# Seven-product layers on one core: more of the sums formed in PSUM, and a new order of the products

## The chip, the cores and the metric

The kernel runs on one core of one Trainium2 chip. The metric is the device time of one execution in microseconds (us). Everything is fp32. The engines are TensorE (PE, with its weight loads as PEld), VectorE (DVE), ScalarE (ACT), GpSimd (POOL) and SyncE (SP), whose queue issues nearly all DMAs.

## The reference

The computation is attention with a threshold, then a Fourier mix with a two-layer channel block on its output (batch 8, 8 heads, 576 rows, 64 columns per head, so 512 columns in all and 2048 hidden ones):

```
scores = q @ k^T / 8; keep those >= max - tau; attn = softmax; x = attn @ v
u  = x + real(fft(fft(x, axis=seq), axis=dim))
un = (u - mean(u)) / sqrt(var(u) + 1e-6)
out = u + relu(un @ w_ch1) @ w_ch2
```

## The kernel before

The attention is worked in 160 steps of 128 query rows for two heads (`scores`, `softmax_first/second/third`, `weights_in_parts`, `values_in_parts`). In each step PE forms scores into a pair of two-bank PSUM tiles (tag `sc`), DVE takes the row maximum (L506), ACT the exponential (L512), DVE the threshold and the sum (L527), ACT the scaling (L540). PE then transposes the weights: one transpose into a tile `pe`, and four into each of two tiles `pw` (L578, L596), which ACT copies out (L584, L598).

The channel block takes 512 rows at a time, in nine groups. Group 0 is multiplied in the ordinary way (`channels`), and in its second half the weights are combined into the left sides of seven-product (Strassen-Winograd) multiplication and stored to device memory in blocks (`w1_forms`, tensor `f1`, 28 blocks; `w2_forms`, tensor `f2`, 49 blocks). Groups 1 to 8 run in `two_level`, called g below. Its first layer has four *parts* of 512 columns; a part has seven *products* of two 256-row halves, 28 in all. Each is a generator step that ends in a `yield`, and is one matmul group of 1.73 us on PE; I call its place in the order a *slot*, 0 to 27. The right sides `t1`, `t2`, `minus_t4`, `t3` are differences of the tokens (`u_form`, L1087). Per part, with P1 to P7 the products, what the layer needs is

```
h00 = relu(P1 + P2)        h01 = relu(P1 + P6 + P5 + P3)
h10 = relu(P1 + P6 + P7 + P4)   h11 = relu(P1 + P6 + P7 + P5)
```

Before the change the order in a part is 1, 2, 5, 6, 4, 7, 3. Products 6 and 7 accumulate on the bank of product 1 (`sum_`); all others take a bank of their own. ACT copies P1, P5, P4 out (L1172, L1174, L1182). DVE adds P2 to `h00`, the bank to `h11` giving `h01`, the bank to both halves `h10, h11` in one 1024-column instruction (`both`, `twice`), and P3 to `h01`: four additions that read PSUM, all on L1100. Three `relu` instructions on ACT follow (L1105). `s1_part` (POOL, L1109) then adds `h01` and `h11`. In the second layer the products have seven inner products each (`L1`, `J`), in two banks per outer product (L1306). Product 1 is copied out by ACT (L1321) and product 2 added to it by DVE (L1323).

All engines run in the order in which the program was written out by hand: `fill` advances the channel block by as many slots as a running budget allows, three times in each attention step, so that about one slot lies between the pieces of the attention. The budget counts what a `yield` reports, 4096 for every slot. Groups 7 and 8 have little or no attention left beside them. All single-bank PSUM tiles, of the attention and of the channel block alike, share the tag `mm` with four buffers. A new tile gets, of the buffers whose last reader was already written out in the program, the one whose last reader came first: in the compiled program 947 of 963 such tiles follow this rule exactly. If that reader has not finished when PE gets there, PE waits.

Of the kernel before, what the change touches and what calls it, by code (L numbers as in the profile page):

```python
# [47 lines left out]
def kernel(  # L48
# [12 lines left out]
    nc = tc.nc  # L61
# [856 lines left out]

    ORDER = (1, 2, 5, 6, 4, 7, 3)
    L1 = (1, 2, 5, 4, 6, 7, 3)
    J = (1, 2, 5, 4, 6, 7, 3)
    HH = HID // 2
# [3 lines left out]
    def w1_forms():  # L928

        quarters = {  # L930
            (i, k): [w1[2 * k + c][:, HH * i : HH * (i + 1)] for c in range(2)]
            for i in range(2) for k in range(2)
        }

        def keep(m, at):
            to = f1[:, :, :].rearrange("p (part m) (c n) -> p m c part n", m=7, c=2)
            for c in range(2):
                nc.sync.dma_start(
                    out=to[:, ORDER.index(m), c],
                    in_=quarters[at][c].rearrange("p (part n) -> p part n", n=256),  # L940
                )

        def form(out_, in0, in1, op=ALU.subtract):
            for c in range(2):
                nc.vector.tensor_tensor(
                    out=quarters[out_][c], in0=quarters[in0][c], in1=quarters[in1][c], op=op
                )
                yield

        keep(1, (0, 0))  # L950
        keep(4, (1, 1))
        yield
        keep(2, (0, 1))
        yield
        yield from form((1, 1), (1, 1), (1, 0), ALU.add)
        keep(5, (1, 1))
        yield from form((1, 0), (0, 0), (1, 0))
        keep(7, (1, 0))
        yield from form((0, 0), (1, 1), (0, 0))
        keep(6, (0, 0))  # L960
        yield from form((0, 1), (0, 1), (0, 0))
        keep(3, (0, 1))
        for _ in range(4):
            yield
        ensure(0)
# [96 lines left out]
    def two_level(g, rows):  # L1062
# [21 lines left out]

        def u_form(out_, in0, in1):
            for c in range(2):
                (nc.vector if g >= NG - 2 else nc.gpsimd).tensor_tensor(  # L1087
                    out=out_[:, c], in0=in0[:, c], in1=in1[:, c], op=ALU.subtract
                )

# [54 lines left out]
                yield  # L1145

        own = l2_forms(1)
        for part in range(4):
            cols = slice(512 * part, 512 * part + 512)
            h00, h01, h10, h11 = (quadrant(k, i)[:, cols] for k in range(2) for i in range(2))  # L1150
            both = hs[:, 4096:8192].rearrange("p (i n) -> p i n", i=2)[:, :, cols]
            sum_ = None
            for at, m in enumerate(ORDER):
                left = block(g, False, 7 * part + at)
                if m in (6, 7):
                    bank = sum_
                else:
                    bank = ps.tile([128, 512], FP32, tag="mm", bufs=4, name="ph")
                if m == 1:
                    sum_ = bank  # L1160
                for q in range(2):
                    for c in range(2):
                        nc.tensor.matmul(  # L1163
                            bank[:, 256 * q : 256 * q + 256].rearrange(
                                "p (two n) -> p two n", two=2
                            ),
                            left[:, 256 * c + 128 * q : 256 * c + 128 * q + 128], right[m][:, c],
                            start=q == 0 and c == 0 and m not in (6, 7), stop=c == 1,
                            skip_group_check=True,
                        )  # L1170
                if m == 1:
                    nc.scalar.copy(h00, bank[:, :])  # L1172
                elif m == 5:
                    nc.scalar.copy(h11, bank[:, :])  # L1174
                elif m == 2:
                    add(h00, bank[:, :])
                    relu(h00)
                    background()
                elif m == 6:
                    add(h01, bank[:, :], h11)  # L1180
                elif m == 4:
                    nc.scalar.copy(h10, bank[:, :])  # L1182
                    background()
                elif m == 7:
                    twice = bass.AP(
                        tensor=bank.tensor, offset=bank.offset,
                        ap=[list(bank.ap[0]), [0, 2], [1, 512]],
                    )
                    add(both, twice)
                    relu(both)  # L1190
                else:
                    add(h01, bank[:, :])
                    relu(h01)
                next(forms, None)
                tick()
                if part == 3 and g > 1 and at in (2, 3, 5):
                    next(own)
                yield 4096
            if g > 1:
                s1_part(part)  # L1200
        for _ in forms:
            pass
        while pending or held:
# [72 lines left out]
        if g < NG - 1:  # L1276
            at_slots(6, (0, 1), [plus(P, v_22, v_u), plus(P, v_21, v_u)])
        else:
            at_slots(6, (0, 0), [plus(V, v_22, v_u), plus(P, v_21, v_u)])
            at_slots(6, (1, 1, 1, 1, 1), gather(V, v_22))  # L1280
            at_slots(6, (2, 2), finish(1, 1, v_22))
            at_slots(6, (2, 2, 3, 3, 3), gather(V, v_21))
            at_slots(6, (4, 4), finish(1, 0, v_21))
            at_slots(6, (4,), [stores(2, 3)])
            w = v_12.rearrange("p (j n) -> p j n", n=128)
            at_slots(6, (4,) * 4, [
                plus(V, w[:, 1:5:3], twice(w[:, 0])), plus(V, w[:, 6], w[:, 2]),
                plus(V, w[:, 6], w[:, 4]), lambda: rows.add(0, slice(256, 384), w[:, 1]),
            ])
            second = bass.AP(  # L1290
                tensor=w.tensor, offset=w[:, 3].offset, ap=[list(w.ap[0]), [-128, 2], [1, 128]]
            )
            at_slots(6, (5,) * 4, [
                plus(V, w[:, 5], w[:, 4]), plus(V, w[:, 2:4], twice(w[:, 5])),
                lambda: rows.add(1, slice(256, 512), second), stores(1),
            ])
        for at, m in enumerate(L1):
            for jn, j in enumerate(J):
                cut = g == NG - 1 and m == 3
                if jn in (0, 4) or cut and jn > 4:  # L1300
                    bank = ps.tile([128, 512], FP32, tag="mm", bufs=4, name="po")
                c0 = 0 if cut and jn > 4 else 128 * (jn % 4)
                to = bank[:, c0 : c0 + 128]
                right_ = block(g, True, 7 * at + jn)
                for s in range(4):
                    nc.tensor.matmul(  # L1306
                        to, lefts[m][j][:, s], right_[:, 128 * s : 128 * (s + 1)],
                        start=(jn in (0, 4) or cut and jn > 4) and s == 0, stop=s == 3,
                        skip_group_check=True,
                    )  # L1310
                if jn in (3, 6) or cut and jn > 3:
                    first, end = (0, 512) if jn == 3 else (512, NV)
                    if cut and jn > 3:
                        first, end = 128 * jn, 128 * jn + 128
                    src = bank[:, 0 : end - first]

                    def here(v):
                        return v[:, first:end]

                    if m in (1, 5, 4):  # L1320
                        nc.scalar.copy(here({1: v_u, 5: v_22, 4: v_21}[m]), src)  # L1321
                    elif m == 2:
                        V.tensor_tensor(out=here(v_11), in0=here(v_u), in1=src, op=ALU.add)  # L1323
                    else:
                        to = here(v_12 if m == 3 else v_u)
                        V.tensor_tensor(out=to, in0=to, in1=src, op=ALU.add)  # L1326
                while held:
                    held.pop(0)()
                held.extend(side.get((at, jn), ()))
                while held and not holding:  # L1330
                    held.pop(0)()
                if jn == 3 and at < 4:
                    rows.load((2, 3, 0, 1)[at])
                    if at == 3:
                        wanted.append(rows)
                    yield ND * 128
                if jn < 6:
                    yield 2048
            background()
            if m != 3:  # L1340
                yield 2048
# [37 lines left out]
    def background():  # L1379

        if late:
            fold_more()
# [361 lines left out]
```

## Time and profile before

| what | value |
|---|---|
| median of 3 runs | 1605.03 us (1603.99 to 1605.74) |
| profiled execution, its time | 1605.7 us |
| span of its instructions | 1603.8 us |
| PE, DVE, ACT, POOL busy | 1537.4, 1105.6, 908.4, 811.7 us |
| first layers of groups 1 to 8 begin at | 386.8, 551.7, 726.9, 900.3, 1074.0, 1247.6, 1400.5, 1498.7 us |
| first layers end at | 460.4, 630.8, 806.8, 979.5, 1153.1, 1326.7, 1452.8, 1547.3 us |

The profile is of one execution; 1.9 us of its time lie outside the span. A line of a group of instructions reads: source line, engine, operation, tile written <- tiles read, shape, count | busy us in total, mean ns of one | idle time of the engine just before them, and what ended most of it. PE's matmuls are pipelined, and the end of a record is modelled: a product of 1.73 us is eight records that overlap. Records carry the tile's name in the program, so `w_all` also stands for rooms that are cut out of the second weight buffer.

### The profile page before, as it was taken

What the parts mean: (1) busy time and instruction counts of PE and PEld (TensorE: products, weight loads), DVE (VectorE), ACT (ScalarE), POOL (GpSimd) and SP (SyncE); (2) the same over time, 40 slices, a digit from 0 to 9 for tenths busy, and PEclk for the clock granted to TensorE, in tenths of its full rate; (3) what the DMA queues carried; (4) which work ended last, traced back from release to release, by engine and by line L of the source; (5) the groups of instructions that cost most, each with busy time, mean ns of one, the idle gap of its engine ahead of it and who ended that gap; (6) DMA issues with size and microseconds to landing.
All of it is one profiled execution on the core that took longest, in us unless ns stands there. A gap on an engine that the chain in (4) does not pass through costs nothing.

```text
span 1603.8 us, 27061 instructions
## 1 busy us (share of the span) xinstructions
PE 1537.4 (96%) x9770; PEld 1189.2 (74%) x9770; DVE 1105.6 (69%) x2165; ACT 908.4 (57%) x1873; POOL 811.7 (51%) x1014
## 2 busy tenths in 40 slices
PE   8999979999999999999999999999999999999997
PEld 4555445555787778877787878787887778879997
DVE  7997886845869566766577566856676656746547
ACT  5774665554655666656666666656665665223121
POOL 6784664034455552536254724455263625537646
PEclk9999999999999999999999999999999999999998
DMA  6423221555956264634564355626463534546655
GB/s 158 131 57 115 75 76 36 175 158 164 291 159 203 72 182 125 182 104 141 141 175 140 113 159 145 191 69 180 123 185 108 154 113 158 191 157 237 235 193 190
DMA packets 245499, 239.05 MB, mean 149 GB/s; under 512 B 196947, under 2 KB 214869, under 8 KB 225014
## 3 DMA queue, kind: packets, MB, share of 16 engines
q1 hardware_dynamic: 242854, 237.02, 49.1%
q8 instruction: 78, 1.28, 0.3%
q10 hardware_dynamic: 2512, 0.30, 0.2%
q14 instruction: 55, 0.45, 0.1%
HBM read 207.50 MB, written 29.62 MB: 148 GB/s over the span
## 4 chain that ended last, share of the span: by engine, by line
PE 76%; DVE 14%; ACT 4%; issue 2%; POOL 2%; DMA 1%; SPq 0%; DVEq 0%; ACTq 0%; POOLq 0%
PE ph L1163 24%; PE po L1306 17%; PE pv L627 8%; PE sc L427 7%; PE pw L596 6%; PE po L901 4%; PE ph L877 2%; PE py L750 2%; DVE e L467 2%; PE sc L433 1%; PE pa L767 1%; PE pe L578 1%; PE pa L771 1%; DVE neg L451 1%; ACT e L512 1%
## 5 line engine op out<-in xcount | busy, mean ns | idle before, releaser
L512 ACT ACTIVATE e<-sc,neg 128x576 f32<-128x576 f32 x216 | 158.6, 734 | 139.8 <-DVE neg L506 139.4
L506 DVE TENSOR_REDUCE neg<-sc 128x1 f32<-128x576 f32 x216 | 154.0, 749 | 112.0 <-PE sc L427 104.1
L1306 PE MATMUL po<-w,w_all 128*128 128x128 f32 x1792 | 229.1, 278 | 0.7 <-ACT ends L584 0.7
L1306 PEld LDWEIGHTS po<-w,w_all 128*128 128x128 f32 x1792 | 214.7, 193 | 10.2 <-issue 5.5
L1100 DVE TENSOR_TENSOR hs<-ph,hs 128x512 f32<-128x512 f32 (+1 forms) x128 | 105.1, 821 | 158.5 <-PE ph L1163 104.0
L1109 POOL TENSOR_TENSOR w<-hs 128x512 f32<-128x512 f32 x32 | 42.1, 1320 | 318.9 <-ACT hs L1105 245.1
L596 PE MATMUL pw<-ident,e 128*128 128x128 f32 x1152 | 172.1, 276 | 18.0 <-ACT x_first L634 9.1
L1163 PE MATMUL ph<-u_t,w 128*128 128x256 f32 x768 | 180.5, 381 | 0.5 <-DMA w<-f 0.4
L527 DVE SCALAR_TENSOR_TENSOR e<-sc,thr,e 128x576 f32<-128x576 f32 x216 | 168.1, 811 | 17.7 <-ACT thr L516 17.7
L427 PE MATMUL sc<-kT,qT 64*128 64x288 f32 x1024 | 170.3, 432 | 7.9 <-DVE e L467 7.9
L598 ACT COPY e_t<-pw 128x512 f32<-128x512 f32 x256 | 148.5, 594 | 45.8 <-PE pw L596 44.6
L540 ACT ACTIVATE e<-e,den 128x576 f32<-128x576 f32 x216 | 157.6, 775 | 16.6 <-DVE den L534 15.4
L596 PEld LDWEIGHTS pw<-ident,e 128*128 128x128 f32 x1152 | 136.3, 142 | 36.3 <-ACT x_first L634 10.1
L1163 PE MATMUL ph<-w_all,w 128*128 128x256 f32 x672 | 157.0, 382 | 2.9 <-DVE hs L1100 1.8
L1163 PEld LDWEIGHTS ph<-u_t,w 128*128 128x128 f32 x768 | 141.2, 190 | 23.4 <-issue 4.4
L1105 ACT ACTIVATE hs<-hs 128x512 f32<-128x512 f32 (+1 forms) x96 | 74.1, 772 | 122.0 <-DVE hs L1100 120.8
L1163 PEld LDWEIGHTS ph<-w_all,w 128*128 128x128 f32 x672 | 123.5, 190 | 25.6 <-issue 6.2
L427 PEld LDWEIGHTS sc<-kT,qT 64*128 64x128 f32 x1024 | 93.9, 186 | 62.9 <-issue 32.8
L1213 POOL TENSOR_TENSOR w_all<-w_all 128x128 f32<-128x128 f32 (+2 forms) x160 | 118.5, 758 | 29.9 <-DVE w_all L1326 22.4
L1306 PE MATMUL po<-w,hs 128*128 128x128 f32 x960 | 126.3, 279 | 0.0
L1306 PEld LDWEIGHTS po<-w,hs 128*128 128x128 f32 x960 | 116.2, 193 | 9.4 <-issue 7.2
L792 POOL TENSOR_TENSOR u_t<-x,tmp 128x289 f32<-128x289 f32 (+1 forms) x45 | 34.5, 766 | 104.8 <-DVE tmp L787 104.8
(221 smaller groups left out, 2985.1 us busy)
## 6 DMA issues: line engine op xcount, KB each, us to landing
w<-f SPq DMA_DIRECT2D x152, 1024.0 KB, 4.9
hs<-in_moe_w_ch_dram SPq DMA_DIRECT2D x23, 512.0 KB, 4.6
q_in<-in_q_dram SPq DMA_DIRECT2D x128, 72.0 KB, 3.9
out_dram<-u SPq DMA_DIRECT2D x36, 256.0 KB, 2.5
k_in<-in_k_dram SPq DMA_DIRECT2D x124, 72.0 KB, 3.0
v_in<-in_v_dram SPq DMA_DIRECT2D x64, 128.0 KB, 4.7
f<-w SPq DMA_DIRECT2D x14, 512.0 KB, 4.0
f<-w SPq DMA_DIRECT2D x7, 1024.0 KB, 4.4
```

The source lines that it names most:

```text
L427: nc.tensor.matmul(sc[j][:, c, 0:HALF], qT[hp, 128 * t : 128 * t + 128], kT[hp, k0 + HALF * c : k0 + HALF * (c + 1)], start=True, stop=True,)
L506: nc.vector.tensor_reduce(out=neg[:, j : j + 1], in_=sc[j][:, :, 0:HALF], axis=AXIS_XY, op=ALU.max, negate=True,)
L512: nc.scalar.activation(out=ej, in_=sc[j][:, :, 0:HALF], func=ACT.Exp, bias=neg[:, j : j + 1], scale=1.0)
L527: nc.vector.scalar_tensor_tensor(out=ej, in0=sc[j][:, :, 0:HALF], scalar=thr[:, j : j + 1], in1=ej, op0=ALU.is_ge, op1=ALU.mult, accum_out ...
L540: nc.scalar.activation(out=e[:, S * j : S * (j + 1)], in_=e[:, S * j : S * (j + 1)], func=ACT.Copy, scale=den[:, j : j + 1],)
L596: nc.tensor.transpose(pw[:, c, :], e[:, c0 : c0 + 128], ident[:, :])
L598: nc.scalar.copy(e_t[:, 4 * j : 4 * j + 4, qs], pw[:, :, :])
L627: nc.tensor.matmul(pv[64 * j : 64 * j + 64, 0:m], vt[:, 2 * c + j, :], e_t[:, 4 * j + c, 0:m] if c < 4 else ends[:, 0, 0:m], start=(c == 0 ...
L1100: nc.vector.tensor_tensor(out=to, in0=bank, in1=to if other is None else other, op=ALU.add)
L1163: nc.tensor.matmul(bank[:, 256 * q : 256 * q + 256].rearrange("p (two n) -> p two n", two=2), left[:, 256 * c + 128 * q : 256 * c + 128 * ...
L1213: return lambda: eng.tensor_tensor(out=to, in0=to, in1=other, op=ALU.add)
L1306: nc.tensor.matmul(to, lefts[m][j][:, s], right_[:, 128 * s : 128 * (s + 1)], start=(jn in (0, 4) or cut and jn > 4) and s == 0, stop=s == ...
```

## The change

1. **Bank of product 1.** P2 is accumulated on it. ACT applies relu straight from the bank into `h00`. ACT has saved P1 to `h10` before, and now copies it from there back into the bank. P6 and P7 follow on it as before.
2. **Bank of product 5.** P3 is accumulated on it after ACT has saved P5 to `h11`; ACT copies the sum to `h01`. P6 is then added to `h01` by DVE.
3. **Order.** It becomes 1 of part 0, then for each part 5, 2, 3, 4, 6, product 1 of the next part (if there is one), 7. So `f1` is stored in this order, with two more cuts: products 1 and 7 take four transfers each in place of two.
4. `t1` is formed on DVE in all groups (before: on POOL in groups 1 to 6).
5. **Second layer.** Product 2 is accumulated on the two banks of product 1, and copied out by ACT where DVE added it.

```diff
-    ORDER = (1, 2, 5, 6, 4, 7, 3)
+    FIRST = [(0, 1)]
+    for part in range(4):
+        FIRST += [(part, m) for m in (5, 2, 3, 4, 6)]
+        FIRST += [(part + 1, 1)] if part < 3 else []
+        FIRST += [(part, 7)]
...
-                (nc.vector if g >= NG - 2 else nc.gpsimd).tensor_tensor(
+                (nc.vector if g >= NG - 2 or out_ is t1 else nc.gpsimd).tensor_tensor(
...
+            left = block(g, False, at)
+            base = {2: 1, 6: 1, 7: 1, 3: 5}.get(m)
+            if base:
+                bank = banks[part, base]
+            else:
+                bank = ps.tile([128, 512], FP32, tag="mm", bufs=4, name="ph")
+                banks[part, m] = bank
...
+                        start=q == 0 and c == 0 and base is None, stop=c == 1,
...
+            if m in (1, 4):
+                nc.scalar.copy(h10, bank[:, :])
...
+            elif m == 5:
+                nc.scalar.copy(h11, bank[:, :])
+            elif m == 3:
+                nc.scalar.copy(h01, bank[:, :])
+            elif m == 2:
+                nc.scalar.activation(out=h00, in_=bank[:, :], func=ACT.Relu)
+                nc.scalar.copy(bank[:, :], h10)
+                background()
+            elif m == 6:
+                add(h01, bank[:, :])
+                relu(h01)
+            elif m == 7:
...
+                add(both, twice)
+                relu(both)
...
+                fresh = jn in (0, 4) or cut and jn > 4
+                if fresh and m == 2:
+                    bank, fresh = firsts.pop(0), False
...
-                    if m in (1, 5, 4):
-                        nc.scalar.copy(here({1: v_u, 5: v_22, 4: v_21}[m]), src)
-                    elif m == 2:
-                        V.tensor_tensor(out=here(v_11), in0=here(v_u), in1=src, op=ALU.add)
+                    if m in (1, 2, 5, 4):
+                        nc.scalar.copy(here({1: v_u, 2: v_11, 5: v_22, 4: v_21}[m]), src)
```

More of the change, by code (lines that the diff above doesn't have):

```diff
@@ L935, in keep @@
         def keep(m, at):
[L936 to L941, printed above, removed]
+            for parts in {1: ((0,), (1, 2, 3)), 7: ((0, 1, 2), (3,))}.get(m, ((0, 1, 2, 3),)):
+                first, last = FIRST.index((parts[0], m)), FIRST.index((parts[-1], m))
+                for c in range(2):
+                    nc.sync.dma_start(
+                        out=f1[:, first : last + 1 : 7, 256 * c : 256 * c + 256],
+                        in_=quarters[at][c][:, 256 * parts[0] : 256 * parts[-1] + 256].rearrange(
+                            "p (part n) -> p part n", n=256
+                        ),
+                    )
         def form(out_, in0, in1, op=ALU.subtract):
@@ L1147, in two_level @@
         own = l2_forms(1)
-        for part in range(4):
+        banks = {}
+        for at, (part, m) in enumerate(FIRST):
             cols = slice(512 * part, 512 * part + 512)
@@ L1151, in two_level @@
             both = hs[:, 4096:8192].rearrange("p (i n) -> p i n", i=2)[:, :, cols]
[L1152 to L1174, printed above, removed]
-                elif m == 2:
-                    add(h00, bank[:, :])
-                    relu(h00)
-                    background()
[L1179 to L1198, printed above, removed]
@@ L1199, in two_level @@
-            if g > 1:
+            left = block(g, False, at)
[5 more added lines that the diff above has]
+                banks[part, m] = bank
+            for q in range(2):
+                for c in range(2):
+                    nc.tensor.matmul(
+                        bank[:, 256 * q : 256 * q + 256].rearrange(
+                            "p (two n) -> p two n", two=2
+                        ),
+                        left[:, 256 * c + 128 * q : 256 * c + 128 * q + 128], right[m][:, c],
+                        start=q == 0 and c == 0 and base is None, stop=c == 1,
+                        skip_group_check=True,
+                    )
@@ new lines, in two_level @@
+            if m in (1, 4):
+                nc.scalar.copy(h10, bank[:, :])
+                if m == 4:
+                    background()
+            elif m == 5:
[10 more added lines that the diff above has]
+            elif m == 7:
+                twice = bass.AP(
+                    tensor=bank.tensor, offset=bank.offset,
+                    ap=[list(bank.ap[0]), [0, 2], [1, 512]],
+                )
+                add(both, twice)
+                relu(both)
@@ L1200, in two_level @@
+            next(forms, None)
+            tick()
+            if g > 1 and (part, m) in ((3, 3), (3, 4), (3, 6)):
+                next(own)
+            if g > 1 and m == 7:
                 s1_part(part)
+            yield 4096
         for _ in forms:
@@ L1296, in two_level @@
             ])
+        firsts = []
         for at, m in enumerate(L1):
@@ L1299, in two_level @@
                 cut = g == NG - 1 and m == 3
-                if jn in (0, 4) or cut and jn > 4:
+                fresh = jn in (0, 4) or cut and jn > 4
+                if fresh and m == 2:
+                    bank, fresh = firsts.pop(0), False
+                elif fresh:
                     bank = ps.tile([128, 512], FP32, tag="mm", bufs=4, name="po")
+                    if m == 1:
+                        firsts.append(bank)
                 c0 = 0 if cut and jn > 4 else 128 * (jn % 4)
@@ L1307, in two_level @@
                         to, lefts[m][j][:, s], right_[:, 128 * s : 128 * (s + 1)],
-                        start=(jn in (0, 4) or cut and jn > 4) and s == 0, stop=s == 3,
+                        start=fresh and s == 0, stop=s == 3,
                         skip_group_check=True,
@@ L1318, in here @@
                         return v[:, first:end]
-                    if m in (1, 5, 4):
-                        nc.scalar.copy(here({1: v_u, 5: v_22, 4: v_21}[m]), src)
-                    elif m == 2:
-                        V.tensor_tensor(out=here(v_11), in0=here(v_u), in1=src, op=ALU.add)
+                    if m in (1, 2, 5, 4):
+                        nc.scalar.copy(here({1: v_u, 2: v_11, 5: v_22, 4: v_21}[m]), src)
                     else:
```

## The prediction

> **What bounds the kernel now.** I read the busy shares first, then the groups of the first layer, then PE's own waits, then the timeline around places where the new order could make PE wait. PE is busy for 96% of the span; DVE and ACT are not close.
>
> ```profile
> PE 1537.4 (96%) x9770; PEld 1189.2 (74%) x9770; DVE 1105.6 (69%) x2165; ACT 908.4 (57%) x1873; POOL 811.7 (51%) x1014
> ...
> L1163 PE MATMUL ph<-w_all,w 128*128 128x256 f32 x672 | 157.0, 382 | 2.9 <-DVE hs L1100 1.8 <-DVE w_all L1087 1.0
> ```
>
> Busy PE need not be PE at its peak, so I looked at the spacing: where no attention lies between, 28 products of groups 7 and 8 follow each other at 1.73 us with no gap. From PE's waits, ranked:
>
> ```profile
> PE pw L596 <- ACT x_first L634: 9.1, 5, 2.2
> PE sc L427 <- DVE e L467: 7.9, 14, 1.7
> PE pe L578 <- DVE w_all L1326: 5.2, 5, 2.6
> ...
> PE ph L1163 <- DVE hs L1100: 2.1, 2, 1.8
> ...
> PE ph L1163 <- DVE w_all L1087: 1.0, 1, 1.0
> PE ph L1163 <- DMA w<-f: 0.4, 1, 0.4
> ```
>
> Of some 54 us of such waits, those in the first layers are 3.5 us (the last three lines). The first and third belong to the seam between batches and to the second layer, the second to the first batches. The change removes no matmul. So relief of DVE can win about 3 us directly, and **the time is decided by whether PE gets new waits**.
>
> [...] at 752.84 a product waits 0.31 us for the DVE addition that empties its bank. [...] the trace's PSUM copies take 576 to 586.
>
> **DVE, ACT, POOL, SP.** Per part, two of the three 512-column additions go (689 ns each): 32 x 2 x 0.689 = 44.1 us. The second layer loses 8 x (0.688 + 0.554) = 9.9. `t1` adds 12 instructions of 0.54 (median of that form, 0.41 to 0.68) = 6.5. DVE ends near 1058. ACT gains per part the copy of product 3 (0.586) and the copy back (0.59[...]); relu of product 2 comes from PSUM (0.597, as L882) instead of SBUF (0.629). 32 x 1.14 = 36.6, plus 8 x (0.587 + 0.476) = 8.5: ACT near 953. POOL loses 12 x 0.724 = 8.7, and was idle 318.9 before L1109 anyway. SP issues 18 stores in place of 14 for `f1`, between 283 and 386; block 0's first use is at 386.8 and its load is issued at 342, so a few tenths there are hidden; bounds 0 and 0.3. All this stands beside PE: nothing on the path.
>
> **New waits of data.** For each product I took the time between the end of the producing product and the start of the consuming slot in this trace, less the queue in front of the copy and the copy. 2 after the copy of 1: 0.9 us or more left over; 3 after the copy of 5: 2.0 or more in groups 1 to 6, some 0.25 in groups 7 and 8 once the 1.06 us relu of 7 before it is counted; 6 after relu and copy back: 3.2 or more in groups 1 to 6, 2.06 in 7 and 8, next to nothing in part 0 of group 7. All are covered. The second layer's product 2 starts 2.3 us or more after product 1's copies end: no wait. **Not covered is 7 right after 6 in part 3** (elsewhere product 1 of the next part lies between): the addition of 6 must end first. Groups 2 to 6: slot 26 ends 1150.80, addition until 1151.58, slot 27 wanted at 1151.18: 0.4 us. Groups 7 and 8, with nothing between: 0.95 each. Group 1: 0.5.
>
> **New waits of banks.** The bank of product 1 is now held from before the previous 7 to its own 7, that of 5 to product 3; mostly two of four are held. The seam of parts 1 and 2 in group 5 shows what that does (PE, DVE and ACT of the timeline):
>
> ```profile
> 1114.35 1.99 PE L1163 MATMUL ph<-u_t,w 128*128 128x256 f32 x8
> 1114.45 1.42 DVE L506 TENSOR_REDUCE neg<-sc 128x1 f32<-128x576 f32 x2 [0.47 <-PE sc L427]
> ...
> 1116.18 0.27 PE L578 MATMUL pe<-ident,e 128*128 128x128 f32 x1
> ...
> 1116.29 0.60 PE L596 MATMUL pw<-ident,e 128*128 128x128 f32 x4
> ...
> 1116.72 1.89 PE L1163 MATMUL ph<-u_t,w 128*128 128x256 f32 x8
> ...
> 1117.79 0.61 ACT L598 COPY e_t<-pw 128x512 f32<-128x512 f32 x1
> ```
>
> The first slot will be 7(1), product 7 of part 1, and the next 5(2). Held: 1(2), product 1 of part 2. `pe` and `pw` take the two free ones, so 5(2) gets the bank of 1(1), whose last reader is the 1.22 us addition of 7(1). That starts at 1116.43 (1116.34, the modelled end, plus the 0.09 seen at other such places) and ends at 1117.65; PE wants the bank at 1116.72. **0.94 us.** The other two would be no better: ACT empties `pw` at 1118.40. By the same bookkeeping over all slots: 4(0) and 4(2) wait 0.31 each for the copy of 3, which they follow closely; and the second layer's first tile lands on the bank of 1(3):
>
> ```profile
> 1151.18 1.89 PE L1163 MATMUL ph<-u_t,w 128*128 128x256 f32 x8
> ...
> 1152.91 0.60 PE L596 MATMUL pw<-ident,e 128*128 128x128 f32 x4
> ...
> 1153.41 0.82 PE L1306 MATMUL po<-w,hs 128*128 128x128 f32 x5
> ...
> 1153.91 0.67 DVE L1100 TENSOR_TENSOR hs<-ph,hs 128x512 f32<-128x512 f32 x1
> ```
>
> The last line is the place of 7(3)'s addition, behind the softmax on DVE; the queue there frees at some 1153.5 once 0.53 us of an earlier addition is gone, and PE too is 0.4 later, so the wait is 1.0. Queued behind DVE's addition is the softmax of the next rows, whose weights PE needs several us later: hidden.
>
> Per group 2 to 6: 0.94 + 0.62 + 0.4 + 1.0 = 3.0; five are 15, and 0.5 more in group 3 (a `pw` behind a `pe`). Group 1, whose seams lie otherwise: 1.45 and 1.35 behind additions and a copy, 0.94, twice 0.31, 0.5 = 4.9. Groups 7 and 8 have no attention between, and the two oldest banks are long free: only the 0.95 each.
>
> **`t1` earlier.** 5 is now slot 1. In group 7 DVE starts `t1` at 1403.12; slot 1 is wanted at 1402.2, so 1.4 us until its first half is ready. But that group's old waits go (0.96 for L1087, 1.83 for L1100). Net -0.4 with the 0.95. In the other groups it is ready within 0.2.
>
> **Sum.** 15 + 0.5 + 4.9 - 0.4 + 0.95 - 0.3 (the wait at 752.84) = 20.7. Group 1's waits partly overlap, since a later PE finds its reader further on; I take off 2. So +18.5 on a span of 1603.8: 1622.3, 1624.2 with the 1.9 around it. The median is 0.7 below the profiled execution: **1623.5 us**, forecast with chance 0.65, its own range 1614 to 1632.
>
> **Rivals.** (A) *The waits are absorbed and DVE's relief wins*, chance 0.23. Place: waits of PE that DVE ends in mid-kernel. For it: 54 us less on DVE before the additions back. Against: ACT, not DVE, ends the largest one. Price: 2.8 (group 7) + 0.3 + up to 5.2 (`pe` behind L1326) - 1.9 (part 3 of groups 7 and 8) = 6.4 won, 1598.5. It decides if the bank waits together stay below about 6 us, that is a third of my 0.94 and 1.0 each. (B) *ACT becomes late*, 0.10. The copy back and the copy of 3 stand before the copies of `pw` in its FIFO; if half of the 32 parts pay 1.1 us more on top: +18, 1641. Against: ACT stays below 60%. (C) *It doesn't do what it says*, since tiles get other banks than I think and never a fresh one: time as before within 2 us, 0.02.
>
> **Chances and range.** A measurement of this kernel can tell about 0.2% (3.2 us) from no change. Slower: 0.65 + 0.10 = 0.75. A's range of 1594 to 1606 lies 0.15 below 1601.8 and 0.08 within; C splits evenly: faster 0.16, same 0.09. Range: the main case with C, the upper part of A and the lower half of B, 1601 to 1635.
>
> **What would show it.** Right: PE's busy time unchanged and its idle some 18 us larger; new rows of PE's waits with DVE `hs` as releaser in front of `ph` and `po`, near 1 us each, once or twice per group, and 0.3 us behind the copy of 3; POOL's wait before L1109 still long. Wrong: PE's idle unchanged, or its new waits ended by ACT's `e_t` or `ends` (B).

## The result and the profile after

The changed kernel takes 1623.43 us (median of 4 runs, 1622.85 to 1625.38) against 1605.26 us for the kernel before (4 runs on the same chip): ratio 1.0117, 95% interval 1.0099 to 1.0134. It is slower by about 18 us; forecast were 1623.5.

First the busy shares of the profile after (1625.4 us, span 1623.5), and the group of the first-layer product that answers to L1163:

```profile
PE 1545.2 (95%) x9770; PEld 1190.9 (73%) x9770; DVE 1078.5 (66%) x2097; ACT 947.2 (58%) x1953; POOL 814.0 (50%) x1002
...
L1169 PE MATMUL ph<-w_all,w 128*128 128x256 f32 x672 | 160.5, 384 | 4.8 <-DVE hs L1107 3.2
```

The number of matmuls is the same. DVE is 27 us lighter, ACT 39 us heavier, and neither matters: PE's idle grew from 66.4 to 78.3 us (span less busy), its busy time by 7.8. Where it waits, from PE's own waits (us in total, times, longest):

```profile
PE sc L427 <- DVE e L467: 10.1, 14, 1.7
PE pw L596 <- ACT x_first L634: 9.1, 5, 2.2
PE ph L1169 <- DVE hs L1107: 8.4, 14, 0.9
PE pe L578 <- DVE w_all L1335: 5.2, 5, 2.6
...
PE ph L1169 <- DVE t_room L1094: 1.2, 1, 1.2
PE ph L1169 <- ACT hs L1184: 0.9, 2, 0.5
...
PE po L1317 <- POOL w_all L1151: 0.4, 2, 0.2
```

The wait for DVE's additions (L1107) was 2.1 us in 2 places and is 8.4 in 14. Two rows of first-layer waits are new: `t1` on DVE (L1094) and the copy of product 3 (L1184). Of the rows above them only the first moved, from 7.9 to 10.1; it lies ahead of the first layers, in the first batches of attention, and stood anywhere between 7.9 and 10.4 in the other runs too. There is no new row in front of `po` with DVE as releaser, which the prediction had expected.

The seam of parts 1 and 2 in group 5, in the timeline of after (start, length, engine, and in brackets the idle before it):

```profile
1128.37 1.99 PE L1169 MATMUL ph<-w_all,w 128*128 128x256 f32 x8
...
1130.31 0.60 PE L596 MATMUL pw<-ident,e 128*128 128x128 f32 x4
1130.40 1.23 DVE L1107 TENSOR_TENSOR hs<-ph,hs 128x1024 f32<-128x1024 f32 x1 [0.51 <-PE ph L1169]
...
1131.68 1.99 PE L1169 MATMUL ph<-t_room,w 128*128 128x256 f32 x8 [0.77 <-DVE hs L1107]
```

Product 5 of part 2 starts 0.05 us after the end of the 1.23 us addition of product 7 of part 1, whose bank it gets. The bracket says 0.77, which is too little, since the end of the record before it is modelled. Starts are better: `pw` to the next product is 0.43 us where nothing is awaited (1116.29 to 1116.72 before), here 1.37. The difference is the forecast's **0.94**.

A smaller wait can show no idle of PE at all. Product 4 of part 2, a little later:

```profile
1141.19 0.60 PE L596 MATMUL pw<-ident,e 128*128 128x128 f32 x4
1141.28 0.59 ACT L1184 COPY hs<-ph 128x512 f32<-128x512 f32 x1 [1.51 <-PE ph L1169]
...
1141.92 1.59 PEld L1169 LDWEIGHTS ph<-w_all,w 128*128 128x128 f32 x8 [0.37 <-ACT hs L1184]
1141.92 1.99 PE L1169 MATMUL ph<-w_all,w 128*128 128x256 f32 x8
```

The product comes 0.73 us after `pw`, so 0.29 are lost, up to the end of the copy at 1141.87; the matmul line has no bracket, only the weight load has.

The end of part 3 in the same group:

```profile
1164.29 1.99 PE L1169 MATMUL ph<-w_all,w 128*128 128x256 f32 x8
...
1166.22 0.60 PE L596 MATMUL pw<-ident,e 128*128 128x128 f32 x4
1166.39 0.69 DVE L1107 TENSOR_TENSOR hs<-ph,hs 128x512 f32<-128x512 f32 x1 [3.42 <-PE pe L578]
...
1167.13 1.99 PE L1169 MATMUL ph<-w_all,w 128*128 128x256 f32 x8 [0.31 <-DVE hs L1107]
1167.65 0.25 ACT L584 COPY ends<-pe 128x128 f32<-128x128 f32 x1
...
1168.96 0.60 PE L596 MATMUL pw<-ident,e 128*128 128x128 f32 x4
...
1169.16 1.23 DVE L1107 TENSOR_TENSOR hs<-ph,hs 128x1024 f32<-128x1024 f32 x1 [0.21 <-PE ph L1169]
...
1169.40 1.06 PE L1317 MATMUL po<-w,hs 128*128 128x128 f32 x8
```

Product 7 comes 0.91 after `pw` and so waits 0.47 for the addition of 6. But the second layer's first tile (last line) comes 0.44 after its `pw`: it waits for nothing, while the addition of 7 is still running.

For all comparisons below I add up the **first layers**: in each group the time from the start of the first product to the end of the last, over eight groups, by the timeline. It is 570.8 us before and 585.6 after:

| group | 1 | 2 | 3 | 4 | 5 | 6 | 7 | 8 |
|---|---|---|---|---|---|---|---|---|
| before | 73.64 | 79.12 | 79.82 | 79.13 | 79.12 | 79.11 | 52.28 | 48.59 |
| after | 76.77 | 81.65 | 81.41 | 81.65 | 81.65 | 81.63 | 51.17 | 49.71 |

That is 14.8 of the 19.7 us between the two spans. The other 4.9 lie where the program is the same or nearly so. About half of it goes with the clock:

- In the clock records, PE is granted half its clock (0.5) in stretches: in before and in after each lasts 3.41 us, some twice that, and one at the very end 11.06 and 9.39. In the 3.41 us ahead of such a stretch PE was idle for 1.1 to 3.0 us; only ahead of the last stretch of after, at the very end of the kernel, was it idle for all of them. Before has 9 such stretches, half of whose length is 20.9 us, after has 11 and 25.2 (the last stretch runs some 2 us past the last instruction in every profile, so each such sum is about 1 us too high). None lies in a first layer of these two.
- The same wait is followed by half clock in one run and not in the other. PE waits 2.19 us for ACT's L634 once in each of groups 3 and 4. In stretches (length, then PE, PEld, DVE, ACT and POOL busy, and PEclk, the granted clock, third from the end) the place in group 3 after the wait reads, in before and in after:

```profile
870.40:873.80 3.40, 3.40 (x27) 2.84 (x26) 3.27 (x9) 3.11 (x7) 0.97 (x1) 1.00 0.00 0
```

```profile
878.90:882.30 3.40, 3.40 (x19) 2.71 (x17) 3.11 (x8) 3.21 (x7) 0.00 (x0) 0.51 0.00 0
```

At full clock PE does 27 matmuls there, at half clock 19. So what follows the first layer is 1.4 us longer in group 3 and 1.0 in group 4, each with 3.41 us more of half clock than in before. Ahead of group 1, where the program is the same but for the stores of `f1`, 1.2 us are lost, also with one stretch more; but other runs of the same program began group 1 anywhere between 386.6 and 389.0 us (half7, with one stretch fewer than before, at 387.8), so this part has no shown cause. The ends of groups 7 and 8 add 0.5 and 1.2, to which an experiment comes back, and the other places take 0.5 off.

### The profile page after: what moved, and what is told of

It reads as the page before. It is cut to its first block, busy times and chain, and to the rows that moved or that the text cites. A ratio compares the mean times of both kernels' runs of the same rounds, so it can differ in the third digit from the quotient of the medians.

```text
span 1623.5 us, 27036 instructions
## 1 busy us (share of the span) xinstructions
PE 1545.2 (95%) x9770; PEld 1190.9 (73%) x9770; DVE 1078.5 (66%) x2097; ACT 947.2 (58%) x1953; POOL 814.0 (50%) x1002
## 4 chain that ended last, share of the span: by engine, by line
PE 72%; DVE 16%; ACT 4%; issue 3%; POOL 3%; DMA 1%; SPq 0%; DVEq 0%; POOLq 0%; ACTq 0%
PE ph L1169 22%; PE po L1317 15%; PE pv L627 8%; PE sc L427 7%; PE pw L596 6%; PE po L901 4%; PE ph L877 2%; DVE e L467 2%; PE py L750 2%; PE sc L433 2%; DVE neg L451 1%; ACT e L512 1%; PE pa L767 1%; DVE e L527 1%; DVE hs L1107 1%
## 5 line engine op out<-in xcount | busy, mean ns | idle before, releaser
L1317 PE MATMUL po<-w,w_all 128*128 128x128 f32 x1792 | 230.5, 279 | 1.2 <-ACT ends L584 0.7
L1317 PEld LDWEIGHTS po<-w,w_all 128*128 128x128 f32 x1792 | 215.6, 194 | 11.1 <-issue 7.1
L1116 POOL TENSOR_TENSOR w<-hs 128x512 f32<-128x512 f32 x32 | 42.1, 1320 | 342.6 <-ACT hs L1112 229.4
L596 PE MATMUL pw<-ident,e 128*128 128x128 f32 x1152 | 173.5, 278 | 17.4 <-ACT x_first L634 9.1
L427 PE MATMUL sc<-kT,qT 64*128 64x288 f32 x1024 | 169.2, 432 | 11.3 <-DVE e L467 10.1
L1169 PE MATMUL ph<-w_all,w 128*128 128x256 f32 x672 | 160.5, 384 | 4.8 <-DVE hs L1107 3.2
L596 PEld LDWEIGHTS pw<-ident,e 128*128 128x128 f32 x1152 | 137.2, 143 | 35.7 <-ACT x_first L634 10.1
L1107 DVE TENSOR_TENSOR hs<-ph,hs 128x512 f32<-128x512 f32 x64 | 61.2, 957 | 141.6 <-PE ph L1169 117.7
L427 PEld LDWEIGHTS sc<-kT,qT 64*128 64x128 f32 x1024 | 93.1, 187 | 66.0 <-issue 36.1
L1317 PE MATMUL po<-w,hs 128*128 128x128 f32 x960 | 125.9, 279 | 0.0
L1317 PEld LDWEIGHTS po<-w,hs 128*128 128x128 f32 x960 | 116.4, 193 | 8.8 <-issue 7.7
L1112 ACT ACTIVATE hs<-hs 128x512 f32<-128x512 f32 x64 | 54.0, 844 | 109.9 <-DVE hs L1107 109.9
```

Source lines behind the costliest of these rows:

```text
L427: nc.tensor.matmul(sc[j][:, c, 0:HALF], qT[hp, 128 * t : 128 * t + 128], kT[hp, k0 + HALF * c : k0 + HALF * (c + 1)], start=True, stop=True,)
L596: nc.tensor.transpose(pw[:, c, :], e[:, c0 : c0 + 128], ident[:, :])
L1107: nc.vector.tensor_tensor(out=to, in0=bank, in1=to if other is None else other, op=ALU.add)
L1169: nc.tensor.matmul(bank[:, 256 * q : 256 * q + 256].rearrange("p (two n) -> p two n", two=2), left[:, 256 * c + 128 * q : 256 * c + 128 * ...
L1317: nc.tensor.matmul(to, lefts[m][j][:, s], right_[:, 128 * s : 128 * (s + 1)], start=fresh and s == 0, stop=s == 3, skip_group_check=True,)
```

## Experiments

All were made on the changed kernel unless said otherwise. Ratios are to the kernel before, run beside them on the same chip (1606.2 to 1607.5 us there). "Lost to the clock" is half the length of the half-clock stretches, as above. It and the first layers are of one profiled execution, the time is a median; in tail the profiled execution took 1610.6 us, 7.7 less than its median.

| run | time, us | ratio [95%] | first layers | lost to the clock |
|---|---|---|---|---|
| before | 1605.3 | 1 | 570.8 | 20.9 |
| after | 1623.4 | 1.0117 [1.0099, 1.0134] | 585.6 | 25.2 |
| second_only | 1606.8 | 1.0000 [0.9989, 1.0010] | 570.3 | 24.4 |
| no_back | 1626.3 | 1.0122 [1.0105, 1.0139] | 585.5 | 28.5 |
| half7 | 1617.4 | 1.0064 [1.0042, 1.0086] | 581.6 | 14.6 |
| tail | 1618.3 | 1.0057 [1.0037, 1.0076] | 578.8 | 14.6 |
| t1_pool | 1637.4 | 1.0193 [1.0165, 1.0222] | 599.2 | 24.5 |
| in_part | 1629.9 | 1.0139 [1.0124, 1.0154] | 593.3 | 20.5 |
| seam | 1644.1 | 1.0230 [1.0206, 1.0254] | 604.1 | 26.4 |
| mend | 1612.3 | 1.0033 [1.0021, 1.0045] | 576.9 | 25.8 |
| p3_own | 1616.3 | 1.0057 [1.0043, 1.0071] | 583.4 | 17.4 |
| mend_own | 1610.4 | 1.0021 [1.0011, 1.0031] | 572.6 | 24.0 |
| forms_dve | 1609.7 | 1.0019 [1.0010, 1.0028] | 572.6 | 28.0 |
| forms_first | 1612.5 | 1.0043 [1.0030, 1.0057] | 577.0 | 22.5 |

### One part alone: the second layer

Product 2 of the second layer accumulated on the banks of product 1, in the kernel before; first layer as before.

> The kernel before with the second layer's edit alone (product 2 on the banks of product 1, copied out by ACT). Waits of PE: no new wait, first layers 571 us, time within 2 us of before. Rival (the two banks held longer starve the attention's transposes): 3 us or more slower.

No effect: DVE falls by 10 us and the time stays. Here relief of an engine that isn't waited for bought nothing, and holding the banks of product 1 in the second layer cost nothing.

### The copy back left out

```diff
-                nc.scalar.copy(bank[:, :], h10)
```

> The changed kernel without the copy of product 1 back into its bank; products 6 and 7 then add to the sum of 1 and 2, so this leaves part of the computation out. ACT has 32 instructions of 0.59 us less, 19 us. Waits of PE: the copy back is hidden, within 2 us of the changed kernel, 1621 to 1625. ACT's added work (rival): 5 us less or more, below 1618.

PE's row of waits for DVE is to the digit that of after, although ACT lost 32 copies of 590 ns:

```profile
PE ph L1169 <- DVE hs L1107: 8.4, 14, 0.9
...
PE ph L1169 <- ACT hs L1184: 1.0, 2, 0.5
```

The first layers are 585.5 against 585.6. The copy back is wholly hidden and ACT's queue isn't the cause (rival B). The time lies 1.3 us above what was expected, with the most half-clock time of all the runs, 28.5 us.

### Half of the addition of product 7

DVE reads the bank once, 512 columns into `h10`; the sum in `h11` is left out.

```diff
-                add(both, twice)
+                add(h10, bank[:, :])
```

> The changed kernel with the addition of product 7 reading its bank once, 512 columns for h10 in place of 1024 for both halves; the sum in h11 is left out. The instruction is 0.53 us shorter. Waits of PE for the bank of product 1: 5(2) waits 0.41 in place of 0.94 in five groups, and once as much less in group 1: 3.2 us less in the first layers (585.6 to 582.4), slot 4 and slot 27 as before. If these places wait for something else than this addition: no change in the first layers.

The group of DVE's additions shows the cut, 690 ns in place of 1223 (first line after, second this run), and PE's row of waits for them falls from 8.4:

```profile
L1107 DVE TENSOR_TENSOR hs<-ph,hs 128x1024 f32<-128x1024 f32 x32 | 39.2, 1223 | 43.8 <-PE ph L1169 38.0 <-PE pe L578 5.7
```

```profile
L1107 DVE TENSOR_TENSOR hs<-ph,hs 128x512 f32<-128x512 f32 x64 | 44.2, 690 | 145.3 <-PE ph L1169 121.5 <-PE pe L578 23.9
```

```profile
PE ph L1169 <- DVE hs L1107: 5.2, 14, 0.9
```

By starts, the wait of product 5 of part 2 falls from 0.94 to 0.40, that is by the 0.53 us that the addition is shorter; those behind the copy of 3 and of 7 behind 6 stay. So the length of the reader of the handed-on bank sets this wait. The first layers fall by 4.0 where 3.2 were expected (group 1 alone gains 1.1). The time fell by more, and this profile lost 10.6 us less to the clock.

### 7 no longer right after 6

```diff
-    for part in range(4):
-        FIRST += [(part, m) for m in (5, 2, 3, 4, 6)]
+    for part, order in enumerate(((5, 2, 3, 4, 6, 7), (5, 2, 3, 4, 6, 7), (5, 2, 3, 4, 6, 7), (5, 2, 3, 6, 4, 7))):
+        FIRST += [(part, m) for m in order[:-1]]
...
-        FIRST += [(part, 7)]
+        FIRST += [(part, order[-1])]
```

(The stores of `f1` are cut by the same list; so in all orders below.)

> The changed kernel with part 3 in the order 5, 2, 3, 6, 4, 7, so that product 4 lies between 6 and 7 as it did before the change. Waits of PE: the waits of slot 27 for DVE go (0.47 in five groups, 0.58 in one, about 1.0 in two), 5 us less than the changed kernel, 1618 to 1619. ACT's added work: no change within 2 us.

```profile
PE ph L1178 <- DVE hs L1116: 4.8, 6, 0.8
```

In this kernel L1178 is the product and L1116 the addition. Eight of the 14 waits are gone, one per group; the five seams of groups 2 to 6 and one in group 1 stay. The first layers fall by 6.8, more than the 5 expected, which were the waits alone: with each of them goes the slow start of the product behind it (some 0.1 us, see below), and group 1 gains 1.5 where 0.58 was counted.

### `t1` on POOL again

```diff
-                (nc.vector if g >= NG - 2 or out_ is t1 else nc.gpsimd).tensor_tensor(
+                (nc.vector if g >= NG - 2 else nc.gpsimd).tensor_tensor(
```

> The changed kernel with t1 formed on POOL in groups 1 to 6, as before the change. Waits of PE: 5 is now slot 1, about 2.2 us earlier than its slot before, when POOL has only just begun t1, so PE waits about 2 us in each of five groups: 8 to 10 us more than the changed kernel, 1632. Rival, that the place of t1 doesn't matter since PE has attention to do first: within 2 us of the changed kernel.

```profile
PE ph L1169 <- POOL t_room L1094: 9.4, 5, 2.2
```

With 5 in slot 1, five groups wait up to 2.2 us for POOL. The first layers grow by 13.6 where 8 to 10 were expected; the new row is 9.4, and two half-clock stretches now fall into first layers. So this part of the change is needed by its order.

### The old way of closing a part

Order 1, 5, 2, 3, 4, 6, 7 in each part: 7 follows 6, product 1 comes after 7, so that only one bank of product 1 is held.

```diff
+    FIRST = [(part, m) for part in range(4) for m in (1, 5, 2, 3, 4, 6, 7)]
```

> The changed kernel with the products in the order 1, 5, 2, 3, 4, 6, 7 within each part, so that product 1 of the next part no longer lies between 6 and 7. Waits of PE (my theory): 7 waits for the addition of 6 in all four parts, 16.9 us summed over the slots of the trace of before, where the changed kernel has some 5; the bank of product 1 is held for fewer slots, so the waits for banks, some 7 us, mostly go. Net about 5 us more in the first layers (585.6 to 590) and in all, 1628. Rival, that the mixed order itself is what costs: back to 1605 to 1612.

```profile
PE ph L1174 <- DVE hs L1112: 12.0, 22, 0.9
```

There are 22 waits on the additions in place of 14, as the theory has it, and first layers of 593.3, above the 585.6 to 590 expected. So product 1 of the next part ahead of 7 does help: by 3.4 us in each of groups 7 and 8, where no attention lies between, but by only 0.24 to 0.44 in groups 2 to 6, where the wait at the seam takes most of the gain back. Group 1 loses 0.5 by it.

### Two attempts at the seam

First, 2 ahead of 5 and 4 ahead of 3 in parts 1 to 3, so that 5 asks for its bank one slot later:

```diff
+    for part, order in enumerate(((5, 2, 4, 3, 6, 7), (2, 5, 4, 3, 6, 7), (2, 5, 4, 3, 6, 7), (2, 5, 4, 3, 6, 7))):
```

> The changed kernel with another order: in parts 1 to 3 product 2, which needs no new bank, comes first and 5 second (2, 5, 4, 3, 6, next 1, 7), in part 0 the order is 5, 2, 4, 3, 6, next 1, 7. So no product that needs a new bank comes right after 7, and 4 doesn't follow 3. Waits of PE (my theory): the waits of 0.94, 0.34 and 0.29 us in groups 2 to 6 and about 2 us in group 1 go, 9 us less than the changed kernel, 1614 to 1615. ACT's added work (rival): the work is the same, so no change within 3 us, 1620 to 1626.

A clear miss in sign: 1644 where 1614 to 1615 were expected. The waits at the seam go, as meant (the row of DVE's additions falls from 8.4 to 3.7; the eight left are 7 behind 6 in part 3), and worse ones come (in this kernel L1187 copies products 1 and 4, L588 empties `pe`):

```profile
PE ph L1178 <- ACT ends L588: 13.2, 9, 1.5
...
PE pw L596 <- ACT hs L1187: 8.0, 12, 0.9
...
PE ph L1178 <- DVE hs L1116: 3.7, 8, 0.9
```

The bank of 5 is now held over 4 to 3. For that stretch products 1, 5 and 4 hold three of four banks. By the bank numbers of the compiled program 4 of part 1 in group 5 gets the bank of the `pe` just ahead of it, and waits 1.63 us by starts for ACT to empty it; after 4 of parts 0 and 2 it is a `pw` that gets the bank of 4 and waits for ACT's copy. The next run keeps 3 ahead of 4, with 2 ahead of 5, and has neither row: so in part 2 it is 4 ahead of 3, and with it the longer hold of 5, that costs, and not 2 ahead of 5.

Second, only where it is needed: part 2 in the order 2, 5, 3, 4, 6 (3 keeps its distance to 5), part 3 as in the run with 7 after 4:

```diff
+    for part, order in enumerate(((5, 2, 3, 4, 6, 7), (5, 2, 3, 4, 6, 7), (2, 5, 3, 4, 6, 7), (5, 2, 3, 6, 4, 7))):
```

> The changed kernel with part 2 in the order 2, 5, 3, 4, 6, next 1, 7 and part 3 in the order 5, 2, 3, 6, 4, 7; parts 0 and 1 as changed. 5 of part 2 comes one product later, when the addition of 7 is done, and is still held for two slots only in all. Waits of PE: the 0.94 in five groups and the waits of slot 27 go; in groups 7 and 8 3 now follows 5 directly and waits 0.9 each. First layers 576 (585.6 in the changed kernel), time 1613 to 1615. ACT's work or the bank count as such: first layers as in the changed kernel or longer.

First layers 576.9 against 576 expected. The seam's 0.94 and the 0.47 of 7 are gone in groups 2 to 6, and no new wait of more than 0.1 is there; the two behind the copy of 3 stay. In groups 7 and 8, and once in group 1, product 3 now waits some 0.8 (0.9 was forecast) for the copy of 5, which it follows directly:

```profile
PE ph L1178 <- ACT hs L1191: 2.1, 3, 0.8
```

### Product 3 in a bank of its own

```diff
-            base = {2: 1, 6: 1, 7: 1, 3: 5}.get(m)
+            base = {2: 1, 6: 1, 7: 1}.get(m)
...
-                nc.scalar.copy(h01, bank[:, :])
+                add(h01, bank[:, :], h11)
```

> The changed kernel with product 3 in a bank of its own again and added to h11 by DVE. My theory: the wait of product 4 in parts 0 and 2 (0.34 and 0.29 in slots 4 and 18 of groups 2 to 6) is the price of product 3 on the bank of 5, since 4 then takes the bank that 3 has just left; with 3 on its own bank, that of 5 is free when 4 wants one. These waits go, some 0.63 a group in groups 1 to 6, the other waits stay: first layers 582 us (585.6 in the changed kernel), time 1619 to 1621. DVE's busy time goes up by some 22 us to 1100, ACT's down by some 18, which costs nothing. Rival: the bank that 3 itself takes is not free, or the addition of 3 holds DVE in front of the addition of 6 or of 7, so the wait only changes place: first layers 585 or more, 1623 or more.

PE's row behind the copy of 3 is gone, that of DVE's additions is again 8.4. By starts, product 4 still loses 0.12 in part 0 (0.34 in after) and 0.08 in part 2 (0.29). First layers 583.4, down 2.2 where 3.6 were expected, since these 0.2 a group stay, and group 1 gains only 0.2. The time fell by more than 2.2, and with 7 stretches at half clock instead of 11 this profile lost 7.8 us less to the clock.

Both mends together (`mend_own`):

> The changed kernel with the orders of the mended version (part 2: 2, 5, 3, 4, 6, next 1, 7; part 3: 5, 2, 3, 6, 4, 7) and product 3 in a bank of its own. My theory: the gains add up, first layers 576.9 less 3.6 = 573, time 1607 to 1610, within 0.2 per cent of the kernel before or just above, since only the waits of group 1, of its first slot and the POOL form at the end of groups 7 and 8 are left. Rival: with 2 ahead of 5 and a third tile for 3, three banks are wanted at the seam and a pe or pw waits as in the order with 5 held long: first layers 580 or more, 1614 or more.

First layers 572.6 against 573 expected, ratio 1.0021: the waits add up, and with both off the first layers are 1.8 us longer than before the change: 1.8 in group 1, 0.65 in each of groups 2, 4, 5 and 6, less 0.4 in group 3 and 2.2 in group 7. This is the best of the orders, and still 0.2% slower than the kernel before.

### The ends of groups 7 and 8

On the last version, two second-layer forms of products 1 and 2 moved from POOL to DVE in these groups:

```diff
+            late = V if g >= NG - 2 and m in (1, 2) else P
...
-                (P, s3, x11, x21, ALU.subtract),
-                (P, s4, x12, s2, ALU.subtract),
+                (late, s3, x11, x21, ALU.subtract),
+                (late, s4, x12, s2, ALU.subtract),
```

> The last version (mended orders, product 3 in its own bank) with the third and fourth second-layer form of products 1 and 2 worked on DVE instead of POOL in groups 7 and 8. My theory: the 0.5 and 1.2 us that what follows the first layers of groups 7 and 8 takes more than in the kernel before (46.43 and 57.79 against 45.93 and 56.58) come from these forms, which now stand behind s1_part of the last part in POOL's queue, which waits for the relu of the last product. With DVE, which is not behind it, PE's wait for POOL in front of po goes, the two stretches come back to 46.0 and 56.6, the time falls by 1.5 us to 1608 to 1610. Rival: the two stretches are longer for another reason (one more half-clock stretch, DVE's queue at the end), they stay within 0.2 us of 46.4 and 57.8, time unchanged.

The row of PE's waits for POOL in front of `po` is gone, and what follows the first layers of groups 7 and 8 falls from 46.43 and 57.79 to 46.01 and 55.76 us (45.93 and 56.58 before the change). The mechanism holds. The size in group 8 is open, since the last stretch at half clock was also shorter (8.2 against 10.5 us). The time does not show it: the ratios of 1.0019 and 1.0021 have overlapping intervals, and this profile lost 4 us more to the clock.

Last, in addition, 2 ahead of 5 in part 0, so that `t1` has a slot more:

```diff
+    for part, order in enumerate(((2, 5, 3, 4, 6, 7), (5, 2, 3, 4, 6, 7), (2, 5, 3, 4, 6, 7), (5, 2, 3, 6, 4, 7))):
```

> As the run before it, and product 2 ahead of 5 in part 0 too, so that t1, which DVE forms at the start of a group, is wanted one slot later. My theory: the 1.36 us wait of slot 1 in group 7 and its 0.13 in groups 2 to 6 go, first layers 570.5 to 571 (572.6 without it), nothing else moves, and the time is that of the kernel before within 0.2 per cent, not better. Rival: with product 5 later the seam of parts 0 and 1 holds a bank more and a pe or pw waits 0.5 to 0.9 in five groups: first layers 575 or more.

```profile
PE ph L1179 <- ACT hs L1188: 3.7, 7, 0.7
```

A miss, and by neither theory's mechanism. Here product 2 directly follows product 1 of part 0, onto the same bank, and waits for ACT's copy of 1 (L1188), 0.4 to 0.9 us by starts: what I had called "0.9 us or more left over" in the prediction is the slot of product 5 between the two. First layers 577.0.

## Why the prediction came out right, and where it didn't

- **Main reading, right.** No matmul is removed, PE bounds, and the time is set by new waits of PE on banks. Of the 19.7 us of span, 14.8 are in the first layers; those waits went away or shrank one by one with the order, the reader's length or the bank, each in the experiment that was aimed at it.
- **0.94 at the seam, right** in place, releaser and size (0.94 by starts, 1.00 in group 3).
- **0.31 each behind the copy of 3, right**: 0.34 and 0.29.
- **7 right after 6: 0.4 and 0.95, a little low**: 0.47 and 1.02. Besides, the product after such a stop takes some 0.1 us longer from its first start to its second half, which no term had. Per group 2, 4, 5 and 6 the forecast for the first layer was 1.96, the measured 2.5: 2.04 in the three kinds of wait, some 0.4 in four such restarts, and the last 0.1 in small delays of product 5 behind `t1` in slot 1 and of 4 where it directly follows 3.
- **The second layer's first tile, 1.0 in five groups, wrong.** It waits for nothing. The step that failed is "lands on the bank of 1(3)": it starts 0.44 us after `pw`, as without a wait, while the addition of 7(3) is still reading that bank. By the bank numbers of the compiled program the tile gets the bank of the `pe` of 1166.12, which ACT's copy leaves at 1167.90; my bookkeeping had that `pe` give its bank back too late. 5 us of the sum were not there.
- **0.5 more in group 3, wrong**: no `pw` waits behind a `pe` in that first layer; only the wait at its seam is 0.06 longer than in the other groups. The wait at 752.84 is gone as forecast: group 3, 0.7 longer than its neighbours before, is 0.2 shorter than they after.
- **Group 1: 4.9 less 2 for overlap = 2.9, measured 3.1**, from single waits of 0.6 and 1.0 rather than 1.45 and 1.35.
- **Groups 7 and 8: `t1` 1.4, measured 1.36; 0.95, measured 1.02**; net in group 7 -1.1 where -0.4 was forecast, in group 8 +1.1.
- **What no term had:** the clock, 4.3 us more lost in this profile than in before's; and the last forms on POOL, which come behind `s1_part` of part 3 now that 7 is the last product, up to 1.7 us at the ends of groups 7 and 8.
- **The recorded sum has a slip**: 20.7 less 2 is 18.7, and the text goes on with 18.5.

So the sum for the first layers without the missing 5 was 20.7 - 2 - 5 = 13.7 (14.8 measured), and 1.1 more there and the 4.9 elsewhere, most of which no term had, made up the 5 and some 1 us beyond. The profiled execution took 1625.4 us where 1624.2 were forecast. The median came within 0.1 us only because it lies 2.0 below the profiled execution here, and 0.7 before: that it is so close is luck.

- **Engines.** DVE was forecast at 1058 and is 1078.5: the additions changed as reckoned (L1107 by -43.9 against -44.1) and `t1` nearly so (+8.2 against +6.5), but the rows of five other DVE lines grew by 1.8 to 4.0 us each, for which no run shows the cause. ACT 947 against 953. POOL was forecast to lose 8.7 and grew by 2.3: its forms of the right sides fell by 6.4, other rows grew. "PE's busy time unchanged and its idle some 18 us larger" was wrong, +7.8 and +11.9. The record of a product after a stop is longer (1.99 us for 1.89), and so are records at half clock (the eight matmuls of L1317 at 880.78 take 1.90 us, those of L1306 at the same place in before 1.16), so part of what is lost counts as busy.
- **Rival A (relief of DVE wins) is out**: by starts the waits for banks come to some 10 us (1.57 in each of groups 2 to 6, 2.3 in group 1), where it needed less than 6, and the second-layer part of the relief alone, 10 of the 54 us, gives 1.0000. **Rival B (ACT late) is out**: without the copy back the first layers are the same. **Rival C is out** for the first layer; for one tile, the second layer's first, it was the truth.

What is not settled: which runs get how many stretches at half clock. The groups of attention repeat every 174.0 us in the run with product 3 on its own and every 176 to 177 in after, and in the clock records of before and of after the starts of all stretches of a profile lie whole multiples of one length, 3.4133 us, apart (before: 461 from the first to the last); 51 times that make 174.1. So in the former, if its stretches keep to such points too, each wait would lie at the same place between two of them, and in groups 3 to 5 none of three waits of 2.19 us was followed by half clock, while in after all three were. With both mends together the period is 174.1 too from group 4 on, and there the same wait in groups 4 and 5 is followed by half clock 1.4 us after its end both times: so the period alone does not decide it, though the place between two points may. This is argued, not shown: nothing here moves the phase alone.

## What to carry to other kernels

Before sums are moved into PSUM to relieve a vector engine, count how many banks are held over each slot, and for each new tile name the last reader of the bank that it gets; with two of four held here, a wait was the remainder of that reader, and with three held over one product the first layers grew by another 18 us (604.1 against 585.6). So lengthening a hold to avoid one wait may cost more than the wait. Where a product accumulates onto a bank that another engine reads or writes, keep one other product between them: without it the waits here were 0.4 to 1.0 us.

## What was unexpected of the hardware

- Up to the last stretch, PE ran at half clock in before and in after for 3.41 us (at times 6.83) after 3.41 us of which it stood idle for 1.1 to 3.0, and the same 2.19 us wait was followed by it in one and not in the other. 14.6 to 28.5 us were lost to half clock in the profiles here, and nine executions of one kernel (tail) took 1609.9 to 1620.0 us, with a mean granted clock of 0.992 in the three shortest and 0.983 to 0.986 in the others. That is more than many of the effects looked for, so small effects were told apart by the first layers and not by the median.
- The round trip through ACT is free here (first layers of 585.6 us with it, 585.5 without): 590 ns for a copy of 512 columns from SBUF back into a bank, and in after, where another product lies between them, no wait of PE is ended by it.
- A restart costs: a product of eight matmuls has a record of 1.99 us after a stop, or after `scores` or `values` (L427, L627), and 1.89 behind transposes or another product.
